# A gated mix of an S5 scan and a GELU network: three of four chunks computed with features on partitions

## The chip, the cores and the metric

The kernel runs on one core of a Trainium2 chip. The metric is the device time of the whole program in microseconds, the median of several runs. The engines are TensorE (PE; PEld is its weight load), VectorE (DVE), ScalarE (ACT), GpSimd (POOL) and SyncE (SP), which issues most of the transfers. TensorE writes to PSUM, in banks of 128 partitions x 512 float32, of which there are eight; a matmul streams the columns of its right operand against a stationary 128x128 left operand.

## The reference

```python
g = sigmoid((x * gate_w).sum(-1, keepdims=True))     # one gate per token
# A: S5 state space layer
Lam_bar = exp(exp(log_dt) * Lam);  B_bar = ((Lam_bar - 1) / Lam)[:, None] * Bmat
Bu = einsum("bld,pd->blp", x, B_bar)
h = Lam_bar * h + Bu[:, t, :]                         # over 2048 tokens
a = 2 * einsum("blp,dp->bld", hseq, Cmat).real + x * Dskip
# B: feed-forward
b = gelu(x @ w1 + b1) @ w2 + b2
out = g * a + (1 - g) * b                             # bfloat16
```

There are 2048 tokens, D = 640 features and as many states, F = 1728 hidden features.

## The kernel before

The tokens go in four chunks of CH = 512. TensorE, VectorE and ScalarE follow an order written by hand: the order in which the Python code calls the operations is the order of each engine's program. A rough clock (`ck`) is kept beside the code, and VectorE's operations wait in a list (`later`) until `let_out` or `dve_now` places them by that clock. GpSimd's and SyncE's programs are ordered by the scheduler. Each engine works through its own program strictly in order; a transfer starts when SyncE reaches it.

The stages, for a chunk c:

- `ssm(c)`: for each of five state tiles ks, ten matmuls (L550) make the real and imaginary input `Bu` in two banks; ScalarE copies them to `bu` (L553), and `scan_ops` queues VectorE's work: a rotation, two scans (L507) and a rotation back, which gives `hs[c]`. GpSimd works out the carry for the next chunk (L514, L516).
- `ff1(c)`: thirteen hidden tiles of 128 features, five matmuls each (L278), then GELU by ScalarE (L283) into `gel[c]`. The last 64 hidden features and the gate's dot product are computed with tokens on partitions (`last_tile`, L300); ScalarE writes the 64 GELUs to `gelN` and the tanh of half the gate's argument to `gz`, and a DMA transposition (L308) turns `gelN` into `gelL`, two tokens' tiles in the two halves of the partitions.
- `gates(c)`: VectorE makes g and 1-g from `gz`, one column per 128 tokens (`gcol`).
- `fin_b(c)`: the second feed-forward product, with tokens on partitions. For each of four token tiles a, thirteen matmuls of 384 columns and thirteen of 256 (L607) run against `w2_sb`; eight half-row matmuls (L623) add the last 64 features. The banks are first filled with b2 by ScalarE (`biased`, L596, from the broadcast `b2bc`). ScalarE scales by 1-g while it evicts to `gb` (L615).
- `fin_a(c)`: the output product of the S5 layer. VectorE first fills a bank with x * Dskip (`seed`, L581, from `xn` with tokens on partitions and the broadcast `Dbc`); twenty matmuls of 320 columns per token tile (L666) add the states' part; VectorE multiplies by g and adds `gb` (L671) into `ot`, and SyncE stores each token tile (L680).
- `fold(ks)`: ScalarE and VectorE fold a complex factor into `CT_re` and `CT_im`, the matrices of `fin_a`. `first_banks` fills two banks ahead of `fin_b`.

What each stage reads is loaded at the start by SyncE, in the order of L135 to L193: among others `w2_sb` (L183), `w2l` (L185), the rest of chunk 0's `xn` (L186, L187; the helper's line is L135), `b2bc`, `Dbc`, the transposed `xT[2]` and `xT[3]`, and `xn[1]`. The order of the stages is in L685 to L709: ssm(0), ff1(1), ssm(1), fin_b(0), ff1(2), fin_a(0), ssm(2), fin_b(1), fin_a(1), ssm(3), ff1(3), fin_b(2), fin_a(2), fin_b(3), fin_a(3); ff1(0) stands before them.

Small parameter vectors come in as rows of 128 (`rows`, L128) of a zeroed tile (`prmA`, `prmB`); a matmul with the identity turns them into columns (L374, L392).

Of the kernel before, what the change touches and what calls it, by code (L numbers as in the profile page):

```python
# [16 lines left out]
P = 128  # L17
# [24 lines left out]
def kernel(  # L42
# [28 lines left out]
    xnp = ctx.enter_context(tc.tile_pool(name="xnp", bufs=2))  # L71
    work = ctx.enter_context(tc.tile_pool(name="work", bufs=2))
    fwork = ctx.enter_context(tc.tile_pool(name="fwork", bufs=4))

    def bank(dtype=F32):
        return ps.tile([P, CH * 4 // (4 if dtype == F32 else 2)], dtype, name="bank")
# [17 lines left out]
    TSIN = const.tile([P, KS, CH], BF16, name="TSIN")  # L94
    ident = const.tile([P, P], BF16, name="ident")
    prmA = const.tile([P, P], BF16, name="prmA")
    NB = KS + KF - 1
    prmB = const.tile([P, P], BF16, name="prmB")
    colA = const.tile([P, 2 * KS], F32, name="colA")
    colB = const.tile([P, NB + KS], F32, name="colB")  # L100
    Dbc = const.tile([P, D], BF16, name="Dbc")
    carry = const.tile([P, 2, KS], F32, name="carry")
    b1x = const.tile([P, F_LAST + 1], BF16, name="b1x")
    gelN = [const.tile([P, H, P], BF16, name=f"gelN{i}") for i in range(2)]
    gelL = [const.tile([P, H, P], BF16, name=f"gelL{i}") for i in range(2)]
    w2l = const.tile([P, D], BF16, name="w2l")
    b2bc = const.tile([P, D], BF16, name="b2bc")
    gz = const.tile([P, NT], F32, name="gz")
# [10 lines left out]
    def load_xn(c, a0=0, a1=TPC, queue=None):  # L119
        if a0 == 0:  # L120
            xn[c] = xnp.tile([P, TPC, D], BF16, name="xn")
        r0 = c * CH + a0 * P
        (queue or nc.sync).dma_start(out=xn[c][:, a0:a1, :], in_=x2d[r0:r0 + (a1 - a0) * P, :].rearrange("(a p) d -> p a d", p=P))
# [10 lines left out]
    def load_x0(queue, a0, a1, d0, d1):  # L134
        queue.dma_start(out=xn[0][:, a0:a1, d0:d1], in_=x2d[a0 * P:a1 * P, d0:d1].rearrange("(a p) d -> p a d", p=P))  # L135
# [31 lines left out]
    rows(nc.gpsimd, prmB[NB:NB + KS, :], A_Lambda_re)  # L167
    rows(nc.gpsimd, prmB[0:KS, :], gate_w)
    nc.gpsimd.memset(b1x[:, F_LAST:F_LAST + 1], 0.0)
    NQ = 5  # L170
    NP = NQ + HC
    tf = const.tile([P, NP], F32, name="tf")
# [10 lines left out]
        nc.sync.dma_start(out=w2_sb[:, k0:k1, :], in_=B_w2[k0 * P:k1 * P, :].rearrange("(kf p) d -> p kf d", p=P))  # L183
    for h in range(2):
        nc.sync.dma_start(out=w2l[h * F_LAST:(h + 1) * F_LAST, :], in_=B_w2[(KF - 1) * P:F, :])  # L185
    load_x0(nc.sync, 0, H, KA * P, D)  # L186
    load_x0(nc.sync, H, TPC, KA * P, D)  # L187
    nc.sync.dma_start(out=b2bc[:], in_=B_b2.rearrange("(o d) -> o d", o=1).to_broadcast([P, D]))
    nc.sync.dma_start(out=Dbc[:], in_=A_Dskip.rearrange("(o d) -> o d", o=1).to_broadcast([P, D]))
    nc.sync.dma_start_transpose(out=xT[2][:], in_=x2d[2 * CH:3 * CH, :])  # L190
    nc.sync.dma_start_transpose(out=xT[3][:], in_=x2d[3 * CH:4 * CH, :])
    for a in range(TPC):
        load_xn(1, a, a + 1)  # L193

    ctx.enter_context(tc.manual_schedule(engines={E.PE, E.DVE, E.Activation}))

# [30 lines left out]
    def act(cost):  # L227
        ck.act = max(ck.act, ck.pe + 0.2) + cost
        return ck.act
# [67 lines left out]
    def last_tile(c, p, pv):  # L297
        for a in range(TPC):
            for kd in range(KD):
                nc.tensor.matmul(p[:, a * NL:(a + 1) * NL], lhsT=xT[c][:, kd, a * P:(a + 1) * P],  # L300
                                 rhs=w1c[kd][:, n1c - NL:n1c], start=False, stop=(kd == KD - 1), skip_group_check=True)
                pe(76)
        nc.scalar.activation(out=gelN[c % 2][:].rearrange("p j (h n) -> p h j n", h=2),
                             in_=pv[:, :, 0:F_LAST].rearrange("p (h j) n -> p h j n", h=2), func=ACT.Gelu_apprx_tanh)
        act(0.45)
        nc.scalar.activation(out=gz[:, c * TPC:(c + 1) * TPC], in_=pv[:, :, F_LAST:NL].rearrange("p a o -> p (a o)"), func=ACT.Tanh, scale=0.5)
        act(0.2)
        nc.sync.dma_start_transpose(out=gelL[c % 2][:], in_=gelN[c % 2][:].rearrange("p a n -> p (a n)"))  # L308

    def ff1(c, k0=0, at={}):  # L310
        for kf in range(k0, KF - 1):
            if kf in at:
                at[kf]()
            p = bank()
            if kf == KF - 3:
                last = last_bank(c)
            for kd in range(KD):
                ff1_mm(p, c, kf, kd)
            ff1_act(p, c, kf)
            let_out(ck.pe)  # L320
        last_tile(c, *last)
        let_out(ck.pe)

    def gel_tile(c):
        gel[c] = gelp.tile([P, KF - 1, CH], BF16, name="gel")
# [21 lines left out]
    FC = FSC[:, KS:2 * KS, NQ:NQ + HB]  # L347
    sq = col("sq", n=NQ * KS)
    cq = col("cq", n=NQ * KS)
    kk = work.tile([P, KS, NP], I32, name="bu", bufs=8)  # L350
    sth, cth = sq[:, 0:KS], cq[:, 0:KS]
    sL, cL = sq[:, KS:2 * KS], cq[:, KS:2 * KS]
    sH, cH = sq[:, 2 * KS:3 * KS], cq[:, 2 * KS:3 * KS]
# [187 lines left out]
    def ssm(c, at={}):  # L541
        hs[c] = hsp.tile([P, 2 * KS, CH], BF16, name="hs")
        for ks in range(KS):
            if ks in at:
                at[ks]()
            bu = work.tile([P, 2, CH], BF16, name="bu", bufs=8)
            for ri, BT in enumerate((BT_re, BT_im)):
                p = bank()
                for kd in range(KD):
                    nc.tensor.matmul(p[:], lhsT=BT[ks >= KSA][:, kd, (ks % KSA if ks < KSA else ks - KSA) * P:][:, 0:P], rhs=xT[c][:, kd, :],  # L550
                                     start=(kd == 0), stop=(kd == KD - 1))
                    pe(CH)
                nc.scalar.activation(out=bu[:, ri, :], in_=p[:], func=ACT.Identity)  # L553
                act(0.6)
            scan_ops(c, ks, bu, ck.act)
            let_out(ck.pe)
# [43 lines left out]
    def first_banks(c):  # L600
        biased(c, "wide", 0)
        biased(c, "wide", 1)

    def fin_b(c, at={}):
        def full(p, col, a, d0, d1):
            for kf in range(KF - 1):
                nc.tensor.matmul(p[:, col:col + d1 - d0], lhsT=gel[c][:, kf, a * P:(a + 1) * P], rhs=w2_sb[:, kf, d0:d1],  # L607
                                 start=False, stop=False, skip_group_check=True)
                pe(d1 - d0)

        def out_of(p, col, a, d0, d1):
            ti = c * TPC + a
            if gbs[ti] is None:
                gbs[ti] = fwork.tile([P, D], F32, name="gb")
            nc.scalar.activation(out=gbs[ti][:, d0:d1], in_=p[:, col:col + d1 - d0], func=ACT.Identity, scale=gcol[:, 1, ti:ti + 1])  # L615
            act(0.56 if d1 - d0 > 320 else 0.45)

        def half_rows():
            for d0, d1 in (MAIN, REST):
                for j in range(H):  # L620
                    for h in range(2):
                        p, col = (opened[c, "wide", h * H + j], 0) if d0 == 0 else (opened[c, "rest", h], j * (D - WIDE))
                        nc.tensor.matmul(p[:, col:col + d1 - d0], lhsT=gelL[c % 2][h * F_LAST:(h + 1) * F_LAST, j, :],  # L623
                                         rhs=w2l[h * F_LAST:(h + 1) * F_LAST, d0:d1], start=False, stop=True, skip_group_check=True)
                    pe(d1 - d0)
            ck.pe += 0.2

        biased(c, "rest", 0)
        biased(c, "wide", 2)
        for h in range(2):  # L630
            for j in range(H):
                a = h * H + j
                full(opened[c, "wide", a], 0, a, *MAIN)
                if a == 0:
                    biased(c, "wide", 3)
                    biased(c, "rest", 1)
                if h == 1:
                    out_of(opened[c, "wide", a], 0, a, *MAIN)
                if a in at:
                    at[a]()  # L640
                let_out(ck.pe)
            for j in range(H):
                full(opened[c, "rest", h], j * (D - WIDE), h * H + j, *REST)
            if h == 0:
                half_rows()
                for j in range(H):
                    out_of(opened[c, "wide", j], 0, j, *MAIN)
            for j in range(H):
                out_of(opened[c, "rest", h], j * (D - WIDE), h * H + j, *REST)
            let_out(ck.pe)  # L650

    def fin_a(c, at={}):
        let_out(0, c)
        for a in range(TPC):
# [24 lines left out]
            if ti < NT - 1:  # L679
                nc.sync.dma_start(out=out2d[ti * P:(ti + 1) * P, :], in_=ot[:])  # L680

    def seeds(c):
        return {2: lambda: seed(c * TPC), 3: lambda: seed(c * TPC + 1)}

    ssm(0)  # L685
    gel_tile(1)
    ff1(1)
    gates(0)
    ssm(1, {KS - 1: lambda: first_banks(0)})
    gates(1)  # L690
    fin_b(0, {a: (lambda a=a: fold(a)) for a in range(3)})
    gel_tile(2)
    ff1(2, 0, {1: lambda: fold(3), 4: lambda: fold(4), 9: lambda: seed(0), 11: lambda: seed(1)})
    gates(2)
    fin_a(0)
    load_xn(2)
    ssm(2, {KS - 1: lambda: first_banks(1)})
    fin_b(1, seeds(1))
    fin_a(1)
    load_xn(3)  # L700
    ssm(3)
    gel_tile(3)
    ff1(3, 0, {KF - 3: lambda: first_banks(2)})
    fin_b(2, seeds(2))
    gates(3)
    fin_a(2, {TPC - 1: lambda: first_banks(3)})
    fin_b(3, seeds(3))
    let_out(1e9)
    fin_a(3)  # L709
# [30 lines left out]
```

## Time and profile before

| what | value |
|---|---|
| median of 3 runs | 214.99 us (214.55 to 215.09) |
| the profiled execution: time, and its span | 215.26 us, 213.5 us |
| ssm(0), L550 | 20.6 to 31.3 us |
| ff1(1), L278 and L300 | 31.3 to 46.0 us |
| fin_b(0), L607 and L623 | 56.8 to 71.6 us |
| fin_a(0), L666 | 86.3 to 97.1 us |
| fin_b(1) and fin_a(1) | 107.9 to 133.7 us |
| fin_b(2) and fin_a(2) | 159.1 to 184.9 us |
| fin_b(3) and fin_a(3) | 184.9 to 210.7 us |
| transfers through SyncE's and ScalarE's queues | 16 MB, most of them before 50 us |

The span runs from the first to the last instruction that the profiler shows; the time of the execution has 1.76 us more around it. The stages follow from the chain that ended last, which lists TensorE's matmuls by line. In the tables of instruction groups a matmul's duration includes its way through the array, so durations overlap; the distance between starts is what one costs.

### The profile page before, as it was taken

The page shows a single profiled execution, that of the slowest core. Times are in us where ns is not written, and L with a number is a line of the kernel's source. Part 1 is how long each engine was busy: PE and PEld are TensorE (multiplying, and loading weights), DVE is VectorE, ACT ScalarE, POOL GpSimd, SP SyncE. Part 2 cuts the span into 40 slices and gives each one's busy share as a digit, 9 for nine tenths or more (in the row PEclk, how much of TensorE's full clock was granted, in tenths as well). Part 3 has the DMA queues.
Part 4 walks back from the last instruction along what each step waited for, and adds up shares of the span by engine and source line. Part 5 has one row for each costly group of instructions (what it writes and reads, how often), then busy time and mean ns, then how long its engine had stood idle before and what let it go on. Part 6 is the DMA issues. An engine that isn't in the chain of part 4 may idle for free.

```text
span 213.5 us, 3592 instructions
## 1 busy us (share of the span) xinstructions
PE 209.3 (98%) x1371; PEld 126.1 (59%) x1382; DVE 183.2 (86%) x335; ACT 102.4 (48%) x184; POOL 62.0 (29%) x101
## 2 busy tenths in 40 slices
PE   8999999999999999999999999999999999999994
PEld 5845444454576644775457777444457587676773
DVE  1579999999998999999999999999999999903153
ACT  3499856665858588203663210456682422205100
POOL 7024069854441563404135503055000000000000
PEclk9999999999999999999999999999999999999999
DMA  6999999995000000061000005100000000100012
GB/s 192 239 176 217 212 240 319 281 221 150 3 0 0 3 0 0 12 186 64 0 0 3 0 2 186 61 0 0 0 3 15 0 3 31 61 34 0 0 63 65
DMA packets 33314, 16.24 MB, mean 76 GB/s; under 512 B 24720, under 2 KB 33296, under 8 KB 33296
## 3 DMA queue, kind: packets, MB, share of 16 engines
q1 hardware_dynamic: 32560, 15.50, 29.5%
q10 hardware_dynamic: 576, 0.49, 0.7%
q8 instruction: 11, 0.18, 0.3%
q14 instruction: 7, 0.06, 0.1%
q0 software_dynamic: 160, 0.01, 0.1%
HBM read 7.48 MB, written 2.62 MB: 47 GB/s over the span
## 4 chain that ended last, share of the span: by engine, by line
PE 98%; issue 0%; DVE 0%
PE bank L607 27%; PE bank L278 27%; PE bank L666 20%; PE bank L550 20%; PE bank L237 1%; PE bank L623 1%; PE bank L300 1%; PE bank L240 0%; DVE ot L671 0%; PE bank L362 0%; PE bank L374 0%; PE bank L392 0%
## 5 line engine op out<-in xcount | busy, mean ns | idle before, releaser
L607 PE MATMUL bank<-w_sb,gel 128*128 128x384 bf16 (+1 forms) x416 | 57.9, 299 | 0.0
L607 PEld LDWEIGHTS <-gel 128*128 128x128 bf16 x416 | 40.3, 98 | 17.0 <-issue 0.8
L553 ACT ACTIVATE bu<-bank 128x512 bf16<-128x512 f32 x40 | 23.6, 597 | 37.5 <-PE bank L550 37.5
L283 ACT ACTIVATE gel<-bank,colB 128x512 bf16<-128x512 f32 x52 | 34.1, 693 | 10.9 <-PE bank L278 10.6
L666 PEld LDWEIGHTS <-hs 128*128 128x128 bf16 x330 | 31.7, 98 | 11.6
L507 DVE TENSOR_TENSOR_SCAN g<-r_c,carry,v 128x512 bf16<-128x512 f32 x30 | 37.2, 1270 | 0.0
L514 POOL TENSOR_SCALAR e<-g,cq 128x2 f32<-128x2 bf16 x15 | 18.3, 1221 | 64.3 <-DVE g L507 64.3
L615 ACT ACTIVATE gb<-bank,gcol 128x384 f32<-128x384 f32 (+1 forms) x32 | 15.1, 525 | 33.8 <-PE bank L623 16.9
L278 PE MATMUL bank<-xT,w1a 128*128 128x512 bf16 (+2 forms) x158 | 28.1, 333 | 0.2
L666 PE MATMUL bank<-CT_re,hs 128*128 128x320 bf16 (+2 forms) x165 | 27.1, 295 | 0.0
L666 PE MATMUL bank<-CT_im,hs 128*128 128x320 bf16 (+2 forms) x165 | 27.1, 295 | 0.0
L671 DVE SCALAR_TENSOR_TENSOR ot<-bank,gcol,gb 128x320 bf16<-128x320 f32 (+2 forms) x33 | 17.4, 531 | 9.6 <-PE bank L666 9.5
L550 PE MATMUL bank<-xT,BT_im 128*128 128x512 bf16 x99 | 24.8, 379 | 0.1
L550 PE MATMUL bank<-xT,BT_re 128*128 128x512 bf16 x97 | 24.4, 379 | 0.2
L278 PEld LDWEIGHTS <-w1a 128*128 128x128 bf16 x162 | 14.9, 104 | 11.8
L581 DVE TENSOR_TENSOR bank<-xn,Dbc 128x320 f32<-128x320 bf16 (+2 forms) x33 | 14.5, 482 | 7.1 <-ACT gb L615 7.1
L278 PE MATMUL bank<-xT,w1b 128*128 128x512 bf16 x80 | 17.9, 379 | 0.0
L550 PEld LDWEIGHTS <-BT_im 128*128 128x128 bf16 x100 | 9.8, 98 | 11.8
L550 PEld LDWEIGHTS <-BT_re 128*128 128x128 bf16 x100 | 9.7, 98 | 11.0
L516 POOL TENSOR_TENSOR carry<-e,e 128x1 f32<-128x1 f32 x30 | 15.7, 546 | 1.3
L488 DVE TENSOR_TENSOR v<-wa,wb 128x512 bf16<-128x512 bf16 x40 | 15.2, 422 | 0.6
L596 ACT ACTIVATE bank<-b2bc 128x384 f32<-128x384 bf16 (+1 forms) x24 | 11.7, 529 | 7.1 <-DVE ot L671 7.1
(110 smaller groups left out, 215.3 us busy)
## 6 DMA issues: line engine op xcount, KB each, us to landing
out_dram<-ot SPq DMA_DIRECT2D x15, 160.0 KB, 1.8
w_sb<-in_B_w_dram SPq DMA_DIRECT2D x2, 640.0 KB, 5.7
xn<-in_A_x_dram SPq DMA_DIRECT2D x2, 640.0 KB, 4.3
w_sb<-in_B_w_dram SPq DMA_DIRECT2D x1, 800.0 KB, 8.5
w1b<-in_B_w_dram SPq DMA_DIRECT2D x5, 128.0 KB, 3.3
xn<-in_A_x_dram SPq DMA_DIRECT2D x4, 160.0 KB, 3.0
w1a<-in_B_w_dram SPq DMA_DIRECT2D x3, 192.0 KB, 2.9
w1a<-in_B_w_dram ACTq DMA_DIRECT2D x2, 192.0 KB, 2.9
```

The lines of the kernel that those rows point to most:

```text
L278: nc.tensor.matmul(p[:, t0:t1], lhsT=w, rhs=xT[c][:, kd, t0:t1], start=(kd == 0) if first is None else first, stop=(kd == last), skip_grou ...
L283: nc.scalar.activation(out=gel[c][:, kf, :], in_=p[:, :], func=ACT.Gelu_apprx_tanh, bias=b1_c[:, kf:kf + 1])
L488: nc.vector.tensor_tensor(out=o, in0=a, in1=b, op=op)
L507: nc.vector.tensor_tensor_scan(s["g"][:, ri, :], r_c[:, ks:ks + 1].to_broadcast([P, CH]), s["v"][:, ri, :], init, ALU.mult, ALU.add)
L514: nc.gpsimd.tensor_scalar(out=t[:], in0=g[:, :, CH - 1], scalar1=f[:, ks:ks + 1], scalar2=None, op0=ALU.mult)
L516: nc.gpsimd.tensor_tensor(out=carry[:, ri, ks:ks + 1], in0=m[0][:, ri:ri + 1], in1=m[1][:, 1 - ri:2 - ri], op=op)
L550: nc.tensor.matmul(p[:], lhsT=BT[ks >= KSA][:, kd, (ks % KSA if ks < KSA else ks - KSA) * P:][:, 0:P], rhs=xT[c][:, kd, :], start=(kd == 0 ...
L553: nc.scalar.activation(out=bu[:, ri, :], in_=p[:], func=ACT.Identity)
L607: nc.tensor.matmul(p[:, col:col + d1 - d0], lhsT=gel[c][:, kf, a * P:(a + 1) * P], rhs=w2_sb[:, kf, d0:d1], start=False, stop=False, skip_ ...
L615: nc.scalar.activation(out=gbs[ti][:, d0:d1], in_=p[:, col:col + d1 - d0], func=ACT.Identity, scale=gcol[:, 1, ti:ti + 1])
L666: nc.tensor.matmul(p[:, 0:d1 - d0], lhsT=hs[c][:, j, lo:lo + P], rhs=CT[:, j % KS, d0:d1], start=False, stop=(j == 2 * KS - 1), skip_group ...
L671: nc.vector.scalar_tensor_tensor(out=ot[:, d0:d1], in0=p[:, 0:d1 - d0], scalar=gcol[:, 0, ti:ti + 1], in1=gbs[ti][:, d0:d1], op0=ALU.mult, ...
```

## The change

For chunks 0 to 2, `fin_b` and `fin_a` are replaced by `fin_b_across` and `fin_a_across`, whose results have features on partitions and 512 tokens along the columns; chunk 3 stays as it was. So the weights are now the stationary operand and the tokens stream. With that

- 1-g and g vary along the columns. `gates_across` stores `gz` to DRAM as a line of 512 numbers right after the chunk's `ff1`; `gates_back` broadcasts the line to all partitions, and GpSimd makes both gates from it (`gate2`, one buffer). VectorE's `gates` stays for chunk 3.
- b2 and Dskip are columns: `prmC` is zeroed by GpSimd, loaded by SyncE in the place of the two loads of chunk 0's `xn`, and turned by a matmul in `skip_columns`, called between `ssm(0)` and `ff1(1)`.
- ScalarE seeds the banks of `fin_a_across` from the transposed x and the Dskip column; it adds b2 while it evicts in `fin_b_across`, and GpSimd multiplies by 1-g.
- VectorE ends a feature tile with two operations, g times the bank and the sum; a DMA transposition turns each 128x512 tile back to tokens on partitions, and one store (two for chunk 2) writes the chunk.
- The loads of xn[1] and xn[2] go; the folds move by one place; `bu` has seven buffers for eight; `gelN` is one tile for two, written twice side by side by a broadcast.

```diff
+    prmC = const.tile([P, P], BF16, name="prmC")
+    colC = const.tile([P, 2 * KD], F32, name="colC")
...
+    nc.gpsimd.memset(prmC[:], 0.0)
...
     for h in range(2):
         nc.sync.dma_start(out=w2l[h * F_LAST:(h + 1) * F_LAST, :], in_=B_w2[(KF - 1) * P:F, :])
-    load_x0(nc.sync, 0, H, KA * P, D)
-    load_x0(nc.sync, H, TPC, KA * P, D)
+    rows(nc.sync, prmC[0:KD, :], A_Dskip)
+    rows(nc.sync, prmC[KD:2 * KD, :], B_b2)
...
-    for a in range(TPC):
-        load_xn(1, a, a + 1)
...
+    def gates_across(c):
+        line = dram.tile([TPC * P], F32, name=f"line{c}")
+        nc.sync.dma_start(out=line[:].rearrange("(a p) -> p a", p=P), in_=gz[:, c * TPC:(c + 1) * TPC])
+    def gates_back(c):
+        g2 = fwork.tile([P, 2, CH], F32, name="gate2", bufs=1)
+        nc.sync.dma_start(out=g2[:, 1, :], in_=line[:].rearrange("(o t) -> o t", o=1).to_broadcast([P, CH]))
+        nc.gpsimd.tensor_scalar(out=g2[:, 0, :], in0=g2[:, 1, :], scalar1=0.5, scalar2=0.5, op0=ALU.mult, op1=ALU.add)
+        nc.gpsimd.tensor_scalar(out=g2[:, 1, :], in0=g2[:, 1, :], scalar1=-0.5, scalar2=0.5, op0=ALU.mult, op1=ALU.add)
...
+    def skip_columns():
+        nc.tensor.matmul(held["c"][:, 0:2 * KD], lhsT=prmC[:], rhs=ident[:, 0:2 * KD], start=True, stop=True)
+        nc.scalar.activation(out=colC[:], in_=held["c"][:, 0:2 * KD], func=ACT.Identity)
+    def seed_across(c, dt):
+        p = bank()
+        nc.scalar.activation(out=p[:], in_=xT[c][:, dt, :], func=ACT.Identity, scale=dskip_c[:, dt:dt + 1])
+    def fin_b_across(c, at={}):
+        p = [(bank(), 0, CH) for _ in range(KD - 1)] + held[c, "cleared"]
...
+        for dt in range(KD):
...
+            for pi, t0, t1 in mine:
+                for kf in range(KF - 1):
+                    nc.tensor.matmul(pi[:, 0:t1 - t0], lhsT=w2_sb[:, kf, dt * P:(dt + 1) * P], rhs=gel[c][:, kf, t0:t1],
+                                     start=False, stop=(kf == KF - 2), skip_group_check=(t1 - t0 < CH))
+                nc.scalar.activation(out=gb[:, t0:t1], in_=pi[:, 0:t1 - t0], func=ACT.Identity, bias=b2_c[:, dt:dt + 1])
+            nc.gpsimd.tensor_tensor(out=gb, in0=gb, in1=gate2[c][:, 1, :], op=ALU.mult)
+    def fin_a_across(c, at={}):
...
+                nc.tensor.matmul(p[:], lhsT=CT[:, j % KS, dt * P:(dt + 1) * P], rhs=hs[c][:, j, :],
+                                 start=False, stop=(j == 2 * KS - 1), skip_group_check=True)
...
+                nc.vector.tensor_tensor(out=t, in0=p[:], in1=gate2[c][:, 0, :], op=ALU.mult)
+                nc.vector.tensor_tensor(out=ot, in0=t, in1=part_b[c, dt], op=ALU.add)
+            nc.sync.dma_start_transpose(out=o4[:, :, dt * P:(dt + 1) * P], in_=ot)
...
     ssm(0)
     gel_tile(1)
+    held["c"] = bank()
+    skip_columns()
     ff1(1)
-    gates(0)
-    ssm(1, {KS - 1: lambda: first_banks(0)})
+    gates_back(0)
+    ssm(1, {KS - 1: lambda: cleared(0)})
...
```

The fifth feature tile of `fin_b_across` is computed in two banks of 256 tokens, which `cleared` zeroes ahead; the last 64 hidden features open all six banks, in pairs of 64 rows.

## The prediction

> **What bounds the kernel now.** I read the busy shares first, then the chain that ended last, then SyncE's queue and the landing times of its transfers, because the change puts new small loads in that queue.
>
> The page's busy shares, and its chain by engine:
>
> ```profile
> PE 209.3 (98%) x1371; PEld 126.1 (59%) x1382; DVE 183.2 (86%) x335; ACT 102.4 (48%) x184; POOL 62.0 (29%) x101
> PE 98%; issue 0%; DVE 0%
> ```
>
> TensorE is the bound: its matmuls are the whole chain, end to end. Only two things can change the time: fewer microseconds of matmuls, or a hole between them. The chain in order of time (start, us, what) has no hole, and shows the start-up and the place where the change inserts a matmul:
>
> ```profile
> 0.76 2.72 PE bank L237 x9
> ...
> 4.66 0.96 PE bank L278 x9
> ...
> 5.83 1.31 PE bank L278 x18
> ...
> 7.26 0.34 PE bank L278 x6
> ...
> 20.58 10.74 PE bank L550 x49
> 31.32 0.22 PE bank L278
> 31.53 0.05 issue
> 31.59 10.74 PE bank L278 x49
> ```
>
> Two things are to be seen. ssm(0) (L550) ends at 31.3 us and ff1(1) (L278) follows at once. And the array starts slow: L237 streams 5x512 + 4x128 = 3072 columns in 2.72 us, 0.89 ns a column, and nine 128-column matmuls from 4.66 take 107 ns each, against 57 ns each from 7.26. The 18 from 5.83 are mixed: 107a + 57(18-a) = 1310 gives a = 5.7, so the rate doubles at about 5.83 + 0.61 = 6.4 us. Half rate from 0.76 to 6.4 is 5.7 us, of which 2.8 are lost.
>
> SyncE's queue in order of time (start, us from first to last issue), and from the DMA issues the KB and median us from issue to landing:
>
> ```profile
> 33.75 1.18 SPq L185 DMA_DIRECT2D w2l<-in_B_w_dram  x2
> 34.98 1.10 SPq L135 DMA_DIRECT2D xn<-in_A_x_dram  x2
> 36.12 0.47 SPq L188 DMA_DIRECT2D b2bc<-in_B_b_dram  x1
> ```
>
> ```profile
> w2l<-in_B_w_dram SPq DMA_DIRECT2D x2, 80.0 KB, 6.9
> xn<-in_A_x_dram SPq DMA_DIRECT2D x2, 192.0 KB, 6.5
> b2bc<-in_B_b_dram SPq DMA_DIRECT2D x1, 160.0 KB, 6.3
> ```
>
> SyncE issues one transfer after another and reaches this place only at 35 us, with the 2.1 MB of w2_sb issued just ahead, from 30.8: whatever is issued here lands 6 to 7 us later.
>
> **The change part by part.**
>
> *The skip and bias columns: the step that decides.* prmC's two loads stand in SyncE's program exactly where the two xn loads stood, behind w2l, and all before them is unchanged. They are issued at 35.0 and 35.5. Their memset on GpSimd stands beside L169's at 4.4 us and hides under the start. `skip_columns` is a matmul that reads prmC, and it stands in TensorE's program between ssm(0) and ff1(1), at 31.3 us. TensorE works in program order, so all of ff1(1), whose data is there, queues behind it; ScalarE's copy to colC and its GELUs follow; colC itself is first needed by fin_b(0)'s evictions, from 60 us on. When does prmC land? Lowest bound: the quickest gelL transposition landed 2.3 us after issue, so 35.5 + 2.3 = 37.8. Highest: 35.5 + 6.9 = 42.4, as w2l. The second w2l, issued about 34.4, landed no earlier than 6.7 later, 41.1; the new loads carry almost nothing and queue right behind it. I take 41.3. The hole is 41.3 - 31.3 = 10.0 us (6.5 to 11.1). The cover that would have hidden it is 10 us of other matmuls between issue point and use; there is none. TensorE has no slack anywhere, so it is paid in full.
>
> *The array after the hole.* The longest idle time of TensorE in this trace is 0.8 us, before its first matmul, so nothing here shows whether it falls back to half rate. The price lies between 0 and the 2.8 us of the start, the only row in which the array comes out of idleness; ff1(1) is just as dense, and 10 us is long, so I take 2.8.
>
> The Trainium skill (TensorE: Matmul & The Clock Gate, "Part 1: The HAM clock gate") speaks against this change: an idle window of about 3.4 us halves the array's clock until a busy window has passed. By it the loss would be an estimated 1.7 to 3.4 us, and the sum below 1.1 lower to 0.6 higher. The row of the start agrees in kind, with 5.7 us at half rate; the profile's granted clock stands at 1.00 there and does not show it.
>
> *Wider matmuls.* Columns are the same (fin_b 33280, fin_a 25600 a chunk), instructions are fewer. ff1(1) gives the price of 512 columns: 65 matmuls from 31.32 to 45.35, 0.216 us each. fin_b: before, 7.06 + 7.17 = 14.23 us in 104 (L607), plus 0.65 for the half rows (L623); after, 52 x 0.216 + 26 x 0.109 = 14.07 (the last tile's two halves at half the price and 1 ns), and the opening streams the same 1280 columns in pairs, 0.6. fin_a: before 10.87 in 80 (L666); after 50 x 0.216 = 10.8. Gain 0.16 + 0.05 + 0.07 = 0.28 a chunk, 0.85 over three, less about 0.1 for the added small matmul (L374's, of that shape, took 0.16): 0.75.
>
> *VectorE.* Out go 24 of 33 seeds (L581, starts 0.40 apart) and 24 of L671 (0.46 apart), 6.9 us a chunk. In come ten 512-wide float32 operations a chunk: between L671's 0.46 for 320 and L476's 0.80 for 640, 0.66 each, 6.6 us. About even, off the chain: chunk 3's states were ready at 185.2 for use at 199.75. But TensorE now waits for VectorE by banks: the eighth bank of ssm(3) is that of fin_a(1)'s fifth tile. Before, the last L671 of fin_a(1) ended at 135.9, 2.2 us after that stage's last matmul; I reckon the same lag, and the bank is wanted 7.5 us in. Margin about 5 us, cost 0. The ring of seven bu buffers for eight asks VectorE to have read chunk 2's third one (122.2 to 124.2) before ssm(3) refills it after 142: cover 18 us, cost 0, and the full lateness if VectorE fell that far back.
>
> *GpSimd.* 15 multiplies and six scalings of 128x512 float32. None is in the trace: by the 0.28 us of the 128x128 affine select at the start, four times as long, 1.1; with the 1.2 us that L514 takes for two elements while VectorE works, 2.3. GpSimd has been idle 71% of the span, and a chunk's seven operations, 8 to 16 us, fit between fin_b and the adds. Cost 0; the high end is in the second rival.
>
> The Trainium skill (SBUF — State Buffer, "Who interferes with whom") says that a GpSimd operation and a VectorE operation with two SBUF inputs exclude each other for a whole instruction. L514's 1.2 us agrees on one side; no row shows VectorE waiting. By it the scans could lose some time with each new operation, and the sum would still be as below while that stays under the margin.
>
> *ScalarE.* Evictions of 128x512 (L553 0.60, L283 0.69), four a chunk, and two half ones, 3.6 us, in place of L615's eight (4.2) and L596's six (3.0); five seeds of 0.6 and two clears of at most 0.5 come in. It is 52% idle; the gelN write is 0.65 for 0.38. The folds shift by one tile: in fin_b(0) an eviction and a fold, 0.69 + 1.64 = 2.3, fit under 2.8 of matmuls. Cost 0; without that cover a delay of at most 0.9 us before TensorE.
>
> *SyncE and DMA.* Per chunk: a gate line out, a broadcast back, five transpositions of 128x512 (gelL's issue 1.17, landing 2.6), one or two stores for four. 5 x 1.2 = 6 us of issue fit into 10.8 of fin_a. The broadcast waits for the line's landing and holds the gelL of the next chunk behind it, some 3 us, needed 10 us or more later. xn(1), xn(2) leave. Cost 0; the last chunk's stores, which end the run, are unchanged.
>
> **The sum.** The profiled execution took 215.26 (span 213.5 and 1.76 around it). 215.26 + 10.0 + 2.8 - 0.75 = 227.3; that execution lies 0.27 above the median of the three runs, 214.99, so 227.0 as a median.
>
> **The rivals.**
> 1. The hole without the slow restart: 227.0 - 2.8 = 224.2. For it: no mid-kernel idling shows a fallback. Against: the 5.7 us at the start.
> 2. VectorE becomes the bound by banks: GpSimd's seven operations for chunk 1, at 1.1 us each of VectorE's time, make 7.7, 2.7 over the margin: 229.7. For it: VectorE is busy without a break from 60 us on. Against: GpSimd is the one that waits in L514's row.
> 3. A short hole: the tiny loads overtake the weights and land 2.3 us after issue. Hole 6.5, 3.5 less than taken: 223.5. Against: all three neighbours took over 6.
> 4. The other side: prmC is there before 31.3, so that only the narrower instruction count shows: 214.99 - 0.75 = 214.2, faster. It decides if the two loads are issued before about 24 us; SyncE's queue, with nothing in front changed, says 35.
>
> **How the numbers follow.** Forecast 0.60, first rival 0.16, second 0.13, third 0.08, fourth 0.03. The range 223.4 to 229.7 takes in the first three rivals as costed, and with them a hole between 6.5 and 11.1; outside lie the fourth rival and some 1 in 10 for what I have not seen. A measurement tells a difference from about 0.3%, 0.65 us: faster 0.02 (the fourth, in part), same 0.01, slower 0.97.
>
> **What would show it.** After: TensorE idle from 31.3 to about 41, released by the DMA of prmC; L278 after it with matmuls 0.43 us apart for some 5 us, then 0.216; fin_b near 14.65 and fin_a near 10.8 a chunk; no waits of TensorE for VectorE in ssm(2) and ssm(3). I am wrong if prmC lands well before 41, or if further holes stand behind it.

## The result, and the profile after

The changed kernel takes 232.2 us (231.0 to 233.66), against 214.77 us for the kernel before beside it: ratio 1.0815, 95% interval 1.0748 to 1.0883. It is slower, as forecast, but by 5.2 us more than the 227.0 forecast, and above the range's end of 229.7. The profiled execution took 232.56 us, its span 230.8, 17.3 more than the 213.5 before.

First the page's busy shares, TensorE's busy tenths and its granted clock in 40 slices (5.8 us each):

```profile
PE 211.1 (91%) x1209; PEld 108.6 (47%) x1209; DVE 197.5 (86%) x311; ACT 105.1 (46%) x182; POOL 86.9 (38%) x123
PE   8999920799999999979999999977999999998995
PEclk9999995699999999999999999999999999999999
```

TensorE's work has hardly grown (209.3 to 211.1); its share fell from 98 to 91%. There is one deep hole (slices 6 to 8), and then three shallow ones, of 7, 77 and 8. And VectorE, whose results are no more than before, is busy 14.3 us longer (183.2 to 197.5).

Every hole and its releaser is in TensorE's timeline (start, us, what, idle time before and who ended it):

```profile
29.17 1.24 PE L574 MATMUL bank<-xT,BT_im 128*128 128x512 bf16 x5
41.70 0.19 PE L710 MATMUL bank<-ident,prmC 128*128 128x10 bf16 x1 [11.29 <-DMA prmC<-in_B_b_dram]
41.74 8.17 PE L283 MATMUL bank<-xT,w1a 128*128 128x512 bf16 x30
...
57.91 1.24 PE L574 MATMUL bank<-xT,BT_re 128*128 128x512 bf16 x5
...
99.24 0.25 PE L305 MATMUL bank<-w1c_lo,xT 128*128 128x65 bf16 x3 [1.49 <-ACT bank L298]
...
153.70 1.24 PE L574 MATMUL bank<-xT,BT_im 128*128 128x512 bf16 x5 [1.10 <-DVE ft L769]
...
157.64 1.24 PE L574 MATMUL bank<-xT,BT_im 128*128 128x512 bf16 x5 [1.32 <-DVE ft L769]
...
209.52 0.38 PE L647 MATMUL bank<-w2l,gelL 64*128 64x256 bf16 x3 [0.63 <-ACT bank L620]
```

The first is the forecast hole: `skip_columns` waits for prmC, and ff1(1) behind it. The others were not forecast: ff1(2) waits for ScalarE, ssm(3) twice for VectorE, and fin_b(3) for a bank that ScalarE fills late.

SyncE's queue in order of time answers to the rows shown before:

```profile
33.10 1.43 SPq L192 DMA_DIRECT2D w2l<-in_B_w_dram  x2
34.64 0.45 SPq L135 DMA_DIRECT2D prmC<-in_A_Dskip_dram  x1
35.14 0.28 SPq L135 DMA_DIRECT2D prmC<-in_B_b_dram  x1
```

Issued at 35.14, landed about 41.6: 6.5 us for 1.2 KB.

The span's 17.3 us by stage, as distances between starts, after minus before. This execution reached the end of ssm(0) 0.9 us earlier (its array left half rate at the start by 4.4 us, where the one before took until 6.4), so of the 11.3 of idleness 10.4 are added time; the small matmul behind it adds 0.2. ff1(1) 16.17 for 14.64: +1.5. ff1(2) 16.33 for 14.64: +1.7. ssm(3) 13.84 for 10.79: +3.0. fin_b(3) 15.78 for 14.88: +0.9. Three fin_b at 14.72 for 14.88 and three fin_a at 10.79 for 10.87: -0.7. Three other stages at +0.1 each: +0.3. Sum 17.3. The forecast's terms cover 10.4 + 0.2 + 1.5 - 0.7 = 11.4 of it (12.05 was forecast); the three stages with waits behind 80 us add 5.6 that it lacks.

What made VectorE slower? In its groups (count | busy, mean ns), first of before, then of after:

```profile
L507 DVE TENSOR_TENSOR_SCAN g<-r_c,carry,v 128x512 bf16<-128x512 f32 x30 | 37.2, 1270 | 0.0
L488 DVE TENSOR_TENSOR v<-wa,wb 128x512 bf16<-128x512 bf16 x40 | 15.2, 422 | 0.6
```

```profile
L531 DVE TENSOR_TENSOR_SCAN g<-r_c,carry,v 128x512 bf16<-128x512 f32 x30 | 39.4, 1347 | 0.0
L512 DVE TENSOR_TENSOR v<-wa,wb 128x512 bf16<-128x512 bf16 x40 | 20.1, 544 | 0.7
```

The same code, the same shapes, the same counts, and longer. GpSimd's multiplies, which are new:

```profile
L747 POOL TENSOR_TENSOR GB<-GB,gate 128x512 f32<-128x512 f32 x15 | 21.4, 1442 | 20.6 <-ACT GB L745 20.6
```

The timeline shows when VectorE is longer; first GpSimd, then VectorE in the same microseconds, and last the same two operations with no multiply beside them:

```profile
137.06 2.68 POOL L747 TENSOR_TENSOR GB<-GB,gate 128x512 f32<-128x512 f32 x2
```

```profile
136.37 0.69 DVE L512 TENSOR_TENSOR wb<-TSIN,bu 128x1024 bf16<-128x1024 bf16 x1
137.09 2.92 DVE L512 TENSOR_TENSOR v<-wa,wb 128x512 bf16<-128x512 bf16 x2
```

```profile
68.87 0.76 DVE L512 TENSOR_TENSOR v<-wa,wb 128x512 bf16<-128x512 bf16 x2
```

Two operations of a rotation, 0.76 us undisturbed, took 2.92 while GpSimd multiplied twice. That is where the second rival had put it, and it is only a coincidence in time so far.

Last, a wait of VectorE that the forecast did not have either, and GpSimd's part in it:

```profile
63.14 2.34 DVE L531 TENSOR_TENSOR_SCAN g<-r_c,v 128x512 bf16<-128x512 f32 x2 [8.41 <-POOL e L538]
```

```profile
61.23 0.62 POOL L330 TENSOR_SCALAR gate<-gate 128x512 f32<-128x512 f32 x1 [20.00 <-DMA gate<-line]
```

Chunk 0's gate line is issued at 47.55, behind two transpositions of x; it and the broadcast back land at 56.1 and 61.2, so GpSimd stands at the scaling of the gates until then, the carries behind it, and VectorE's next scans behind these, for 8.4 us.

### The profile page after: what moved, and what is told of

Read it like the earlier page. It is cut to its first block, busy times and chain, and to the rows that moved or that the text cites. A ratio compares the mean times of both kernels' runs of the same rounds, so it can differ in the third digit from the quotient of the medians.

```text
span 230.8 us, 3262 instructions
## 1 busy us (share of the span) xinstructions
PE 211.1 (91%) x1209; PEld 108.6 (47%) x1209; DVE 197.5 (86%) x311; ACT 105.1 (46%) x182; POOL 86.9 (38%) x123
## 5 line engine op out<-in xcount | busy, mean ns | idle before, releaser
L742 PE MATMUL bank<-gel,w_sb 128*128 128x512 bf16 (+1 forms) x234 | 42.7, 344 | 0.0
L288 ACT ACTIVATE gel<-bank,colB 128x512 bf16<-128x512 f32 x52 | 34.0, 695 | 11.9 <-PE bank L283 11.8
L742 PEld LDWEIGHTS <-w_sb 128*128 128x128 bf16 x234 | 22.7, 98 | 20.2 <-issue 1.0
L747 POOL TENSOR_TENSOR GB<-GB,gate 128x512 f32<-128x512 f32 x15 | 21.4, 1442 | 20.6 <-ACT GB L745 20.6
L745 ACT ACTIVATE GB<-bank,colC 128x512 f32<-128x512 f32 (+1 forms) x18 | 11.1, 615 | 25.5 <-PE bank L742 21.7
L512 DVE TENSOR_TENSOR v<-wa,wb 128x512 bf16<-128x512 bf16 x40 | 20.1, 544 | 0.7
L531 DVE TENSOR_TENSOR_SCAN g<-r_c,v 128x512 bf16<-128x512 f32 x10 | 11.7, 1207 | 8.4 <-POOL e L538 8.4
L762 PE MATMUL bank<-hs,CT_re 128*128 128x512 bf16 x75 | 18.6, 379 | 0.0
L762 PE MATMUL bank<-hs,CT_im 128*128 128x512 bf16 x75 | 18.6, 379 | 0.0
L574 PEld LDWEIGHTS <-BT_im 128*128 128x128 bf16 x100 | 9.8, 98 | 14.6 <-issue 3.0
L512 DVE TENSOR_TENSOR wa<-TCOS,bu 128x1024 bf16<-128x1024 bf16 x20 | 15.8, 789 | 0.0
L512 DVE TENSOR_TENSOR wb<-TSIN,g 128x1024 bf16<-128x1024 bf16 x20 | 14.7, 737 | 0.0
```

Source lines behind the costliest of these rows:

```text
L288: nc.scalar.activation(out=gel[c][:, kf, :], in_=p[:, :], func=ACT.Gelu_apprx_tanh, bias=b1_c[:, kf:kf + 1])
L512: nc.vector.tensor_tensor(out=o, in0=a, in1=b, op=op)
L531: nc.vector.tensor_tensor_scan(s["g"][:, ri, :], r_c[:, ks:ks + 1].to_broadcast([P, CH]), s["v"][:, ri, :], init, ALU.mult, ALU.add)
L742: nc.tensor.matmul(pi[:, 0:t1 - t0], lhsT=w2_sb[:, kf, dt * P:(dt + 1) * P], rhs=gel[c][:, kf, t0:t1], start=False, stop=(kf == KF - 2), s ...
L747: nc.gpsimd.tensor_tensor(out=gb, in0=gb, in1=gate2[c][:, 1, :], op=ALU.mult)
L762: nc.tensor.matmul(p[:], lhsT=CT[:, j % KS, dt * P:(dt + 1) * P], rhs=hs[c][:, j, :], start=False, stop=(j == 2 * KS - 1), skip_group_chec ...
```

## The experiments

Three things are suspected: the hole (H), chunk 0's gate line in front of the carries (G), and the multiplies' effect on VectorE (M). "Before" and "after" in the table are the kernel before and the changed kernel. Ratios are to the kernel before on the same chip.

| run | what differs | us | ratio (95%) |
|---|---|---|---|
| e1 | before + H alone | 227.16 | 1.0568 (1.0527 to 1.061) |
| e2 | after without H | 229.24 | 1.0674 (1.0609 to 1.0738) |
| e3 | after without G | 232.99 | 1.0843 (1.0811 to 1.0875) |
| e4 | without H and G, first form | 221.46 | 1.0303 (1.0273 to 1.0334) |
| e5 | without H and G | 223.57 | 1.0404 (1.0376 to 1.0432) |
| e6 | without H, G and M | 214.82 | 0.9998 (0.9975 to 1.0021) |
| e7 | before + GpSimd multiplies | 227.4 | 1.0585 (1.0553 to 1.0617) |
| e8 | without H; VectorE evicts, line sent early | 222.5 | 1.0353 (1.0303 to 1.0403) |
| e9 | without H and G; VectorE evicts | 215.4 | 1.0028 (1.0012 to 1.0044) |
| e10 | after without M | 226.2 | 1.0539 (1.0498 to 1.0581) |

### e1: the hole by itself

The kernel before with prmC's memset, its two loads and the small matmul with its copy, placed as in the changed kernel:

```diff
+    rows(nc.sync, prmC[0:KD, :], A_Dskip)
+    rows(nc.sync, prmC[KD:2 * KD, :], B_b2)
     load_x0(nc.sync, 0, H, KA * P, D)
...
     gel_tile(1)
+    pc = bank()
+    nc.tensor.matmul(pc[:, 0:2 * KD], lhsT=prmC[:], rhs=ident[:, 0:2 * KD], start=True, stop=True)
+    nc.scalar.activation(out=colC[:], in_=pc[:, 0:2 * KD], func=ACT.Identity)
+    act(0.2)
     ff1(1)
```

> The kernel before, with only prmC, its two loads at the place they have after the change (the xn loads follow them) and the small matmul between ssm(0) and ff1(1); nothing else of the change, and the output stays the reference's. Theory, the hole is paid in full and the array restarts slow: ssm(0) ends at 31.3, prmC lands at 41.7 as in the trace after, so 10.4 of idle TensorE plus the 1.5 us that ff1(1) took longer there (16.17 for 14.64): 214.8 + 11.9 = 226.7, and no other wait of TensorE. Rival, part of the hole is made up later because VectorE has run ahead meanwhile: under 222. Rival, the hole also disturbs VectorE's or ScalarE's order later: over 229.

227.16 us, +12.3 us. TensorE's timeline:

```profile
40.34 0.19 PE L693 MATMUL bank<-ident,prmC 128*128 128x10 bf16 x1 [9.29 <-DMA prmC<-in_B_b_dram]
```

There is no other wait of note: 9.3 us of hole, and ff1(1) takes 16.1 us from 40.34 for 14.64. In its row of the granted clock the two slices at the hole's end read 5 and 6 as well. So the hole is paid in full and nothing is won back later. VectorE loses the same time: its groups are as before, but it waits 9.64 us for a fold, since the folds stand behind TensorE's program.

### e2: the hole taken away

```diff
-    held["c"] = bank()
-    skip_columns()
     ff1(1)
+    held["c"] = bank()
+    skip_columns()
```

> The changed kernel with the small matmul on prmC called after ff1(1) instead of before it; all else is kept. The hole and the slow restart, 11.3 + 1.5 = 12.8 us, go. Theory A, TensorE alone sets the time: 232.2 - 12.8 = 219.4. Theory B, VectorE is a second bound close behind, since it stands still 8.4 us (54.7 to 63.1) until GpSimd has read g, whatever TensorE does: only the 3.8 us go that VectorE waited for the folds' ScalarE part, and TensorE waits for banks at the end instead: its fin_b(3) would begin near 185 and want the third tile's bank near 191.6, VectorE frees it near 204.5: 226 to 229.

229.24 us: 3 us less than the changed kernel, where the hole is worth 12. What was under the hole came to light (TensorE's timeline):

```profile
78.78 1.24 PE L283 MATMUL bank<-xT,w1a 128*128 128x512 bf16 x5 [2.02 <-ACT GB L745]
92.38 1.44 PE L283 MATMUL bank<-xT,w1c_lo 128*128 128x512 bf16 x3 [6.97 <-ACT gel L288]
```

VectorE still waits 7.83 us for the carries at 63 us, but TensorE is now ten us further on. ScalarE stands up to 8.1 us at a fold that VectorE reaches late, ff1(2)'s GELUs stand behind it, and TensorE's banks behind these. Behind the wait of 6.97 the array runs at half rate again, for 5 us: from 92.38 to the end of ff1(2) 2.6 us are lost by that alone. So the loss is near theory B's number, but not in its place: nearly all of it comes in ff1(2), and fin_b(3), where the theory had it, waits 0.63 us. The hole and the gate line are two delays that lie side by side: each hides most of the other.

### e3, e4 and e5: the gate line taken out of the carries' way

In e3 chunk 0's gates are scaled by ScalarE ahead of fin_b(0)'s third tile, so that the carries don't queue behind them on GpSimd (the first two tiles are multiplied before the scaling there, and in e4); e4 is e3 with e2's edit.

```diff
+        gate2[c] = g2
+        if c == 0:
+            return
         nc.gpsimd.tensor_scalar(out=g2[:, 0, :], in0=g2[:, 1, :], scalar1=0.5, scalar2=0.5, op0=ALU.mult, op1=ALU.add)
...
+    def gates_scaled(c):
+        g2 = gate2[c]
+        nc.scalar.activation(out=g2[:, 0, :], in_=g2[:, 1, :], func=ACT.Identity, scale=0.5, bias=half[:])
+        nc.scalar.activation(out=g2[:, 1, :], in_=g2[:, 1, :], func=ACT.Identity, scale=-0.5, bias=half[:])
...
+            if dt == 2 and c == 0:
+                gates_scaled(c)
```

> The changed kernel, hole and all, but the two scalings of chunk 0's gates are made by ScalarE in fin_b(0) before its third tile, and not by GpSimd in front of the carries. Theory: GpSimd's wait for the gate line (41.2 to 61.2) held the read of g, and so VectorE for 8.4 us; without it VectorE is earlier by that, and TensorE's later waits (ff1(2) 1.5, ssm(3) 2.4, fin_b(3) 1.05, 5.4 with what goes with them) vanish: 226.5 to 227.5, which is what was forecast. Rival, the later waits come from GpSimd's multiplies slowing VectorE (its instructions took 14 us more in total than before): the 8.4 us stall is gone but the time stays above 230.

> Both edits: the small matmul after ff1(1), and chunk 0's gates scaled by ScalarE. Theory B carried on: VectorE, then busy without a break, would end the last bank of fin_a(2) at about 212.4 - 8.4 - 3.8 = 200, while TensorE without holes wants the third tile's bank in fin_b(3) at 191.6 and gets it near 196: 4 to 5 us of waits are left, 218 to 219.5. Rival, hole and gate wait are all there is: 214 to 215.

e3 missed: 232.99 us, no gain, as its rival said. VectorE's 8.4 us are gone, and in their place stands the wait for the folds, as in e1:

```profile
73.74 0.89 DVE L509 SCALAR_TENSOR_TENSOR CT_re<-CT_re,c2re,ft 128x640 bf16<-128x640 bf16 x1 [10.43 <-ACT ft L505]
```

With the hole there, G costs nothing; TensorE's later waits are as long as before (1.01 and 1.49 in ff1(2), 1.13 and 1.32 in ssm(3), 0.63 in fin_b(3)), so G was not their cause. e4, 221.46 us, was also some 2 us over its 218 to 219.5: with H and G both away the same five waits remain, 1.16, 1.50, 1.11, 1.32 and 0.63. Its theory had them all in fin_b(3).

e5 is e4 with the scaling ahead of the first eviction, where every product is with the scaled gate:

```diff
-            if dt == 2 and c == 0:
-                gates_scaled(c)
...
+                if dt == 0 and c == 0:
+                    gates_scaled(c)
                 nc.scalar.activation(out=gb[:, t0:t1], in_=pi[:, 0:t1 - t0], func=ACT.Identity, bias=b2_c[:, dt:dt + 1])
```

> As e4_both, but the scaling of chunk 0's gates stands before the first eviction of fin_b(0), so that all five tiles are multiplied by 1-g (in e3 and e4 the first two were multiplied before the scaling). It is the base of the next run. Expected 220 to 221.5, as e4 with 221.5: TensorE waits for VectorE in ssm(3), for ScalarE in ff1(2) and in fin_b(3), some 5 us together. If the scaling's place mattered: 219.

223.57 us, 2 us over: ScalarE waits 4.5 us for the gate line before that eviction, and TensorE 2.52 where e4 had 1.16. VectorE's busy time is as in the changed kernel:

```profile
PE 209.7 (95%) x1192; PEld 109.3 (49%) x1209; DVE 197.2 (89%) x312; ACT 105.7 (48%) x184; POOL 88.0 (40%) x121
```

Against e2's 229.24, G without a hole above it is worth 5.7 us by e5 and 7.8 by e4, the half rate behind e2's long wait included.

### e6: the multiplies taken away

e5 without GpSimd's 15 multiplies (the factor 1-g is left out of the result):

```diff
-            nc.gpsimd.tensor_tensor(out=gb, in0=gb, in1=gate2[c][:, 1, :], op=ALU.mult)
             part_b[c, dt] = gb
```

> e5 without GpSimd's fifteen multiplies: the factor 1-g of the feed-forward part of chunks 0 to 2 is left out, nothing else. Theory C, what is left over after hole and gate wait is VectorE held up by GpSimd's multiplies (its scans, rotations and folds of the same count and shape took 14 us more in the run after than before): VectorE's total falls from 197.5 to about 184, TensorE's waits vanish, 214 to 215.5. Rival D, the ten result operations a chunk and their place in VectorE's order cost it: VectorE's total falls but TensorE still waits in ssm(3) and fin_b(3), 218 to 220.

214.82 us, no difference from the kernel before. The busy shares:

```profile
PE 208.9 (97%) x1192; PEld 109.7 (51%) x1209; DVE 183.4 (85%) x312; ACT 105.3 (49%) x184; POOL 69.8 (33%) x106
```

Nothing of VectorE's program was touched, and it is 13.8 us shorter (197.2 to 183.4): 0.92 us for each multiply. The two groups shown before, `v` and the scans, are back at 440 and 1281 ns. The kernel gains 8.75 us, and of the five waits one, of 1.21 in ff1(2), is left (in the profiled execution, the longest of ten). This is no coincidence in time any more.

### e7: multiplies added to the kernel before

```diff
             act(0.56 if d1 - d0 > 320 else 0.45)
+            if c < NCH - 1 and d0 > 0:
+                nc.gpsimd.tensor_tensor(out=spare[:], in0=gbs[ti][:, 0:CH], in1=gbs[ti][:, D - CH:D], op=ALU.mult)
```

Twelve multiplies of 128x512, into a tile that nobody reads.

> The kernel before, to which GpSimd does twelve multiplies of 128x512 float32 more, four a chunk, of the evicted gb into a spare tile that nothing reads. Theory C: VectorE's instructions that lie beside them get longer by up to the 1.3 us of a multiply, about 0.9 each on average as after (14 us for 15): VectorE's total rises from 183.2 by 8 to 12; TensorE does not wait, since VectorE's states are 14.6 us early: 214.5 to 216. Rival: the longer VectorE instructions came from something else (the transfers, ScalarE): VectorE's total stays within 2 us.

VectorE's part came as expected, 1.0 us for each multiply, although no instruction of VectorE reads what they write:

```profile
PE 212.6 (94%) x1371; PEld 125.8 (56%) x1382; DVE 195.4 (87%) x335; ACT 102.3 (45%) x184; POOL 80.4 (36%) x113
```

The time did not: 227.4 us, 12.3 more. I had read 14.6 us of slack from the stretch between chunk 3's states and their use; there is none of that kind. VectorE's program holds the seeds that fill fin_a's banks, in their places among the scans, and those of fin_a(2) come late (TensorE's timeline, and its granted clock in slices):

```profile
85.69 1.44 PE L279 MATMUL bank<-xT,w1c_lo 128*128 128x512 bf16 x3 [1.07 <-ACT gel L284]
...
183.68 1.49 PE L669 MATMUL bank<-CT_re,hs 128*128 128x320 bf16 x5 [5.09 <-DVE bank L582]
```

```profile
PEclk9999999999999996999999999999999958999999
```

TensorE's waits for VectorE and ScalarE make 5.5 + 2.5 us here. After the one of 5.09 the starts of five-matmul groups lie 1.3 us apart for three groups, where 0.68 is normal: another 2 us, with the clock at 5 and 8. In ff1(2) the clock falls as well (the 6), and some 1.5 us more are lost. That makes 11.5 of the 11.8 us of span.

How much slack there was stands in the trace of before: VectorE has no idle time of note from 65 to 186 us, fin_a(2)'s first seed (171.38, 0.50 us) is done at 171.9, and its bank is used at 173.83. That is 1.9 us. 12.2 us more of VectorE less 1.9 leave 10.3, and counted from the start of ff1(2) fin_a(2) begins 10.3 us later in e7 than in before.

### e8 and e9: the product moved to VectorE's eviction

If the multiply costs VectorE 0.92 us anyway, VectorE can do it. In both, VectorE evicts fin_b_across's banks, (bank + b2) times 1-g, in one operation, and GpSimd's multiply and ScalarE's eviction go; `skip_columns` stands as in e2. In e8 chunk 0's line goes out and back through ScalarE's queue, right after ff1(0) and ff1(1); in e9 it goes through SyncE's as in the changed kernel, and ScalarE scales it ahead of the first eviction.

```diff
-                nc.scalar.activation(out=gb[:, t0:t1], in_=pi[:, 0:t1 - t0], func=ACT.Identity, bias=b2_c[:, dt:dt + 1])
-                act(0.6)
-            nc.gpsimd.tensor_tensor(out=gb, in0=gb, in1=gate2[c][:, 1, :], op=ALU.mult)
+                def f():
+                    nc.vector.scalar_tensor_tensor(out=gb[:, t0:t1], in0=pi[:, 0:t1 - t0], scalar=b2_c[:, dt:dt + 1],
+                                                   in1=gate2[c][:, 1, t0:t1], op0=ALU.add, op1=ALU.mult)
+                dve_now(ck.pe + 0.2, 0.66 if t1 - t0 == CH else 0.4, f)
```

```diff
-        nc.sync.dma_start(out=line[:].rearrange("(a p) -> p a", p=P), in_=gz[:, c * TPC:(c + 1) * TPC])
+        (nc.scalar if c == 0 else nc.sync).dma_start(out=line[:].rearrange("(a p) -> p a", p=P), in_=gz[:, c * TPC:(c + 1) * TPC])
...
```

> The changed kernel with the small matmul after ff1(1); chunk 0's gate line sent and fetched by ScalarE's queue right after ff1(0) and after ff1(1); and in fin_b_across VectorE evicts, (bank + b2) times (1-g) in one operation, in place of ScalarE's eviction and GpSimd's multiply. Theory C: VectorE gains the 14 us and pays 15 operations of 0.66, about 10: its total near 193, no long GpSimd operation beside it, 214 to 216, at best 0.3% under the kernel before. Rival D: VectorE's order makes TensorE wait all the same, 217 to 221.

> The changed kernel with the skip columns turned behind ff1(1), chunk 0's gates scaled by ScalarE ahead of fin_b(0)'s first eviction, and no multiplies on GpSimd: VectorE evicts fin_b_across's banks itself, (bank + b2) * (1-g) in one operation. The gate line goes out and comes back through SyncE's queue, as in the changed kernel. Theory C (the multiplies' contention is what is left of the loss, and what spoiled the earlier run with VectorE's evictions was the line's transfer in the load phase): 214 to 217, VectorE's busy time about 193, no wait of TensorE over 2.6 us, and the transfers' throughput before 45 us as in the changed kernel. Rival (VectorE's program, with evictions put in among its scans, holds TensorE by banks): 219 or more, with waits of L283 or the fin stages for VectorE.

e8 missed, at 222.5 us, for a reason of its own: a line of 512 numbers of four bytes, whose store is issued at 20.6 us, among the loads of the start. Its throughput by slice (5.5 us each), and the first of TensorE's waits:

```profile
GB/s 179 253 222 216 162 17 103 285 281 156 149 46 0 0 0 3 0 48 48 95 124 0 0 0 26 167 95 119 0 0 27 0 0 3 45 54 145 3 60 60
```

```profile
33.05 6.65 PE L283 MATMUL bank<-xT,w1a 128*128 128x512 bf16 x29 [2.41 <-DMA xT<-in_A_x_dram]
```

From 27 to 38 us it moves 48 GB/s, where the changed kernel moves 274, with its transfer engines no less busy, and SyncE is held 12.0 us at the transposition of CT_im, for 3.9 there; xT, the weights and prmC come late. Behind 70 us TensorE has no wait at all. In e9, with the line back in its old place, the same stretch has 286 GB/s: 215.4 us, as theory C said. Whether the early store or its queue did the harm, the two runs don't tell apart. In e9 the longest wait of TensorE after the start is 0.34 us; the three fin_b across take 14.72 and the three fin_a 10.8, which is the change's own gain of 0.7. It is lost again, 0.5 at ff1(2) and 0.1 at each of three other stages.

### e10: the forecast's terms, and no multiplies

The changed kernel with e6's edit alone (the factor 1-g left out again): H and G stay.

> The changed kernel without GpSimd's 15 multiplies by 1-g and nothing else changed (that factor is left out of the result): the hole at the skip columns, the slow restart and the gate line's wait all stay. Theory C (the forecast's terms were right but for the multiplies, which it priced at nothing): 226 to 228, the forecast's 227; VectorE's busy time 183 to 185; the waits of TensorE in ssm(3) for the rotated states gone. Rival (the 8.4 us wait of VectorE for GpSimd, which is busy with the gates, costs time of its own behind the hole): 229 to 231.

226.2 us, where the forecast for the whole change was 227.0. VectorE's wait of 8.4 us for the carries is still there and costs nothing. TensorE's only waits after the start, in us, times and longest:

```profile
PE bank L710 <- DMA prmC<-in_B_b_dram: 10.1, 1, 10.1
...
PE bank L283 <- issue: 0.2, 1, 0.2
```

and VectorE's groups are back:

```profile
L531 DVE TENSOR_TENSOR_SCAN g<-r_c,carry,v 128x512 bf16<-128x512 f32 x30 | 37.4, 1280 | 0.0
L512 DVE TENSOR_TENSOR v<-wa,wb 128x512 bf16<-128x512 bf16 x40 | 15.9, 439 | 0.7
```

So the multiplies are worth 232.2 - 226.2 = 6.0 us of the changed kernel, the 5.2 that the forecast lacked and a little more.

## Why the prediction was right and wrong

**The hole: right.** Its place, its releaser and its price came as worked out. prmC landed at about 41.6 for 41.3, and 10.4 us of idleness were added for 10.0. e1 shows that nothing hides or returns it.

**The slow restart: right in kind, taken at its upper end.** The idleness does halve the array's rate, which the first rival denied. It cost 1.5 us in the profiled executions of the changed kernel and e1, 2.6 in e3, and 2.9 in e10, whose profiled execution was the longest of its four; 2.8 was forecast. The granted clock, which did not show the slow start of the kernel, shows this one: 0.50 from 36 to 42 us, 0.64 to 46, 1.00 from there. The estimate from the Trainium skill (TensorE: Matmul & The Clock Gate, "Part 1: The HAM clock gate"), 1.7 to 3.4 us, holds 2.6 and 2.9 and is a little over 1.5.

**Wider matmuls: right.** 0.16 us a fin_b and 0.08 a fin_a, 0.7 over three chunks for the 0.85 less 0.1 forecast.

**GpSimd "cost 0", and VectorE's "margin about 5 us": the step that failed.** The multiply's own duration was inside the bounds (1.44 us for 1.1 to 2.3). What the sum put at nothing is that it takes time from VectorE: 0.92 us each, 13.8 in all. The prediction's own paragraph on the skill allowed for this, and the second rival named it and had the price of one about right (1.1), but set one chunk's seven operations against a margin read from one bank of ssm(3). Neither held. The forecast reckoned that fin_a(1)'s products end 2.2 us after that stage's last matmul, and that the bank of the fifth is wanted 7.5 us in. In the changed kernel the fifth comes 10.4 us after:

```profile
156.92 0.67 DVE L769 TENSOR_TENSOR ft<-bank,gate 128x512 f32<-128x512 f32 x1
```

In e10, without the multiplies, it comes 4.3 us after, so the margin was 3.2 us. All three chunks' multiplies push VectorE back, and the lateness comes out at four places: through ScalarE's folds and GELUs in ff1(2), through banks twice in ssm(3), and in fin_b(3) through ScalarE's bank fills, which wait up to 11.9 us for fin_a(2)'s products because these stand behind chunk 3's last scans in VectorE's program. In the kernel before, the margin at fin_a(2)'s seeds was 1.9 us (e7). I had taken one stage's slack for the engine's; "busy without a break from 60 us on" was the line to believe. The 0.13 given to this rival was too little; and the five chances add up to 1.00, so that the "1 in 10 for what I have not seen" had no room in them.

The Trainium skill (SBUF — State Buffer, "Who interferes with whom") states that VectorE and GpSimd share a port pair under an exclusive lock, and that a VectorE instruction with two SBUF inputs contends with a GpSimd instruction that reads SBUF. The runs agree with it and add the price: the instructions that got longer (scans, rotations, and in e7 seeds and folds) all have two SBUF inputs. Whether instructions with one SBUF input are spared is not tested. e9 fits it as well: with VectorE's own evictions in place of the multiplies, `v` is back at 460 ns and the scans at 1270.

**SyncE and DMA "cost 0", "some 3 us": right in the sum, wrong in the working.** The gate line's round trip took 13.7 us, and 8.4 of it stopped VectorE. It cost nothing because it lay under the hole (e3, e10); without the hole it costs 5.7 to 7.8 us (e2 against e5 and e4). The forecast had named the gelL behind the broadcast as what is late, and not the carries behind GpSimd's scaling.

**ScalarE "cost 0"**: its own work fits, but it hands VectorE's lateness on: the waits of ff1(2) and fin_b(3) are for ScalarE, and go when the multiplies go (e10). One of 1.21 us in ff1(2) stays in e6; its cause is not shown.

The change without its three faults (e9) is within half a per cent of the kernel before, 1.0028 (1.0012 to 1.0044), and not faster; the 0.7 us won by wider matmuls does not come through. No version here beats the kernel before.

## What to carry to other kernels

GpSimd's idle share is no free room while VectorE is busy: price an elementwise operation on SBUF tensors that is moved to GpSimd as time of VectorE as well (here 0.92 us for a 1.44 us multiply), and ask what VectorE's program feeds. The slack of an in-order engine is the smallest over all the places that wait for it, not the one at the end of its last job. And when one large wait is found, look for the others that lie under it: e2 took away a hole worth 12 us and gained 3.

## What the runs showed of the hardware that was not expected

Storing 512 numbers of four bytes took 8.2 to 8.7 us from issue to landing in the changed kernel. In e8, with the first such store issued at 20.6 us from ScalarE's queue, the throughput from 27 to 38 us was 48 GB/s in place of 274; which of the two did it is not shown. A load of 1.2 KB issued behind 2.1 MB of weights in the same queue landed 6.5 us after issue, much as the weights did (5.2 to 7.9).

The rate of the array fell to half after idle times of 9.3 to 11.3 us, after one of 7.0 (e2) and one of 5.1 (e7), and also after shorter ones: the granted clock was 0.50 from 52 to 54 us in e8, after a wait of 2.58, and 0.60 and 0.55 from 85 to 89 us in e7, after waits of 1.43 and 1.07 close together. It stayed at 1.00 in e5, after 2.52 and 1.49.
